# Moving one batch's attention two steps within another batch's feed-forward steps

## The chip, the core and the metric

The kernel runs on one core of a Trainium2 chip. The metric is the device time of one execution in microseconds, given as the median of several runs. The core has five engines that run side by side and wait for each other through semaphores: TensorE (PE in the profile, with its weight loads as PEld), VectorE (DVE), ScalarE (ACT), GpSimd (POOL) and SyncE (SP), which issues most transfers. Each engine works through its own instructions strictly in the order in which the kernel issues them. PSUM is the memory that TensorE writes its results to; SBUF is the large on-chip memory.

## The reference

Two parts follow each other: a cross attention between tokens and a small state, and a feed-forward block with `h * cos(h)` between its two matrices.

```python
# x: (8, 8, 512, 64)  state: (8, 8, 32, 64)
scores = scale * np.matmul(x, state.transpose(0, 1, 3, 2))
a = softmax(scores)                       # over the 32 states
xread = np.matmul(a, state)
scores2 = scale * np.matmul(state, x.transpose(0, 1, 3, 2))
a2 = softmax(scores2)                     # over the 512 tokens
sread = np.matmul(a2, x)
x2 = concatenate([xread, sread], axis=2)  # then (B, H, S, D) -> (B*S, H*D) = (4352, 512)

h = x2 @ w_in                             # (512, 2048)
g = h * np.cos(h)
return g @ w_out                          # (2048, 512)
```

(The softmax is written out in the reference, with the maximum subtracted and 1e-9 added to the sum.)

## The kernel before

The kernel goes through the 8 batches. A batch has 16 steps, one for each *tile* of 128 of the 2048 hidden features (by 512 tokens). In the steps of batch `b` it also does, piece by piece, the attention of batch `b + 1`. A plan says which piece falls into which step. This plan is what the change edits:

```python
        def early(b, s):
            if b == 1:
                ...
            else:
                for k in range(NK):                 # 32x32 transposes of the loaded tokens
                    to = (x_dve, y_dve)[k % 2]
                    to[s[k // 2]].append((b, "tokens_turned", k))
            pe[s[2]].append((b, "scores"))
            x_dve[s[2]].append((b, "max1"))
            x_dve[s[3]].append((b, "spread1"))
            y_dve[s[3]].append((b, "shift"))
            x_dve[s[4]].append((b, "max2"))
            y_act[s[4]].append((b, "exps"))
            x_dve[s[5]].append((b, "sums"))
            y_dve[s[5]].append((b, "spread1"))
            x_dve[s[6]].append((b, "norm1"))

        def late(b, s):
            pairs(s[0], b, "turn", "turn_kept", 0)  # turn a2 on TensorE, copy on ScalarE
            pe[s[1]].append((b, "reads", 0))        # sread
            pe[s[2]].append((b, "reads", 1))
            x_dve[s[2]].append((b, "keep"))
            if len(s) > 3:
                turned(b, s[3])                     # keep2 on TensorE, keep3 on ScalarE
        ... # cut: batch 0
            prod(0, b, 1, *[MAIN for _ in bank])
            prod(4, b, 2, *bank)
            prod(9, b, 3, *bank)
            if b + 1 < B:
                prod(13, b + 1, 0)
                early(b + 1, (1 + (b == 1), 2 + (b == 1), 5, 6, 7, 8, 9))
                late(b + 1, (10, 11, 12, 15))
```

`prod(s, b, nt)` is a *state product*: in step `s`, state times a quarter of `w_in` for batch `b`, 16 passes on TensorE into the two PSUM buffers `at`, copied by ScalarE into the buffer `sw` (two of them in turn). Scores, the turned a2 and the reads use the same two buffers `at`; the scores stay there until `exp2` has read them.

The steps of a batch come in two kinds. From batch 2 on, the hidden products of most tiles are done for two tiles at once with seven products in place of eight (Strassen's scheme; in the trace L514), with sums on VectorE; their result is put together in SBUF. The last 8 steps of an odd batch do one plain product (L471) per tile, which stays in PSUM:

```python
    hps = ctx.enter_context(tc.tile_pool(name="hps", bufs=2, space=PSUM))

    def hidden(t):                                   # L471, plain tile
        t.hp = hps.tile([P, S], F32, name="h")[:, 0:t.n]
        ...
    def gate(t):     # L567, ScalarE: q = int(h + 0.25)
    def gate2(t):    # L570, VectorE: q = q - h
    def gate3(t):    # L573, ScalarE: q = sin(pi/2 - 2 pi q)
    def gate4(t):    # L580, VectorE: g = h * q   (the last reader of h)
```

The feed-forward output is a Strassen scheme too, over pairs of batches. Its sums are the subtractions of L586, some on VectorE and some on GpSimd (all on GpSimd in the first pair, batches 0 and 1). The output products are L624; a step has 4 or 8 passes of them (128x128 by 512), three steps behind the tile. Results leave through 32x32 transposes on VectorE (L651) and transfers.

For a pair's first batch the differences of the attention matrix that the seven products need are made ahead by `halves`:

```python
    def halves(b):                                   # L493
        aT = aT_of[b]
        ...
        for i, x1, x2 in ((0, b12, b11), (1, b22, aS[:, 0]), (2, b22, b12),
                          (3, b21, aS[:, 1])):
            nc.vector.tensor_tensor(aS[:, i], x1, x2, op=ALU.subtract)
```

One step of the loop, cut to its order:

```python
    for step, t in enumerate(all_tiles):
        s = step % NF
        ...
        ahead = all_tiles[step + 1:step + 3]
        if seven(t):
            if t.f % 2 == 0:
                hidden_b(t); sums_b(t)               # second half of a pair
        elif step != 1:
            hidden(t)
        first = len(ahead) > 1 and seven(ahead[0]) and ahead[0].f % 2 == 0
        if first:
            if not seven(t):
                h = t.hp
                take_slot(t)
                nc.scalar.copy(t.g, h)               # L957: frees the PSUM buffer early
            hidden_a(*ahead)                         # first half of the next pair
        ...
            go(0)                                    # pe pieces of the plan
            gate(t); gate2(t)
            if first:
                sums_a(ahead[0])
            go(1); go(3)                             # x_act and x_dve pieces
        gate3(t)
        if later:
            later.pop(0)()                           # a piece of a store
        for u, new in zip(all_tiles[step + 2:step + 4], (False, True)):
            if seven(u) and u.f % 2 == 0 and new_pair(u) == new:
                sw_sums(u)
        gate4(t)
        sums(t)                                      # L586
        go(2); go(4)                                 # y_act and y_dve pieces
        for u in all_tiles[step + 5:step + 6]:
            if seven(u) and new_pair(u):
                halves(u.b)
        sums2(t)                                     # L586 on GpSimd
        while len(line) >= (LAG if step >= 2 * NH else LAG + 1):
            output(line.pop(0))                      # L624
        line.append(t)
```

When `reads(1)` of a batch is issued, the loads of the following batch's tokens are issued too, into the buffer that the reads have just used (`xT`) and into `x_b`.

Of the kernel before, what the change touches and what calls it, by code (L numbers as in the profile page):

```python
# [21 lines left out]
def kernel(  # L22
# [10 lines left out]
    B, H, S, D = x.shape  # L33
# [419 lines left out]
    def part(b, name, *args):  # L453

        if b not in attn:
            attn[b] = Attention(b)
        getattr(attn[b], name)(*args)
        if (name, args) == ("reads", (1,)) and b + 1 < B:
            if b > 0:
                attn[b + 1] = Attention(b + 1)  # L460
                attn[b + 1].load_tokens()
            load_x(b + 1)
# [16 lines left out]
    def seven(t):  # L479
        return t.pair is not None and t.b > 1 and t.phase < 3  # L480
# [35 lines left out]
    def take_slot(t):  # L516
        t.slot = g_free.pop(0)
        t.hp = t.g = g_all[:, t.slot, 0:t.n]
# [253 lines left out]
    def tiles():  # L772
        pr = None
        for b in range(B):
            if b % 2 == 0:
                pr = Pair(b // 2, pr)
            for f in range(NF):
                t = Tile()
                t.b, t.f, t.pair = b, f, pr
                t.phase, t.i = b % 2 * 2 + f // NH, f % NH  # L780
                t.n, t.kn = S, 2
                c = slice(P * f % WC, P * f % WC + P)
                t.lhs = lambda i, b=b, nt=P * f // WC, c=c: (
                    sw_of[b, nt][:, i, c])
                t.rhs = lambda i, b=b: aT_of[b][:, i]
                yield t
        for n in range(NF):
            t = Tile()
            t.b, t.n_th, t.f = B, n, (n + NH) % NF
            t.pair, t.last_pair, t.phase = None, pr, None  # L790
            t.n, t.kn = B * Ns, NK
            cols = slice(P * t.f, P * t.f + P)
            t.lhs = lambda i, cols=cols: w_in[:, i, cols]
            t.rhs = lambda i: sT[:, :, Ns * i:Ns * i + Ns]
            yield t


    def warm(n, to):

        for _ in range(n):  # L800
            nc.tensor.matmul(out=to, lhsT=zeros[:, 0:P], rhs=zeros, start=True,
                             stop=True)
# [33 lines left out]
    def plan(b):  # L836
        pe, x_act, y_act, x_dve, y_dve = [
            {s: [] for s in range(NF)} for _ in range(5)]

        def prod(s, b, nt, *bank):  # L840
            pe[s].append((b, "products", nt) + bank)
            if b == 1 and 0 < nt < 3:
                x_dve[s].append((b, "products_taken", nt) + bank)
            else:
                x_act[s].append((b, "products_kept", nt) + bank)

        def pairs(s, b, name, kept, i):
            pe[s] += [(b, name, i), (b, name, i + 1)]
            x_act[s].append((b, kept, i))
            y_act[s].append((b, kept, i + 1))  # L850

        def early(b, s):
            if b == 1:
                pairs(s[0], b, "tokens", "tokens_kept", 0)
                pairs(s[1], b, "tokens", "tokens_kept", 2)
            else:
                for k in range(NK):
# [13 lines that stand above are left out]
            pairs(s[0], b, "turn", "turn_kept", 0)  # L871
            pe[s[1]].append((b, "reads", 0))
# [3 lines that stand above are left out]
                turned(b, s[3])  # L876

        def turned(b, s):
            pe[s].append((b, "keep2"))
            x_act[s].append((b, "keep3"))  # L880


        if b == 0:
            pe[0].append((0, "products", 0, SIDE, HC, WC))
            y_dve[0] += [(0, "products_taken", 0, SIDE, HC, WC),
                         (0, "inverse2")]
            prod(7, 0, 2, SIDE)
            prod(11, 0, 3)
            prod(13, 1, 0, MAIN)
            late(0, (1, 2, 3, 4))  # L890
            early(1, (5, 6, 7, 8, 9, 10, 11))
            late(1, (12, 13, 14))
        else:
            bank = (SIDE,) if b == 1 else ()
            if b == 1:
                turned(1, 0)
            prod(0, b, 1, *[MAIN for _ in bank])
            prod(4, b, 2, *bank)
            prod(9, b, 3, *bank)
            if b + 1 < B:  # L900
                prod(13, b + 1, 0)
                early(b + 1, (1 + (b == 1), 2 + (b == 1), 5, 6, 7, 8, 9))
                late(b + 1, (10, 11, 12, 15))
        return pe, x_act, y_act, x_dve, y_dve

# [20 lines left out]
    all_tiles = list(tiles())  # L926
    for step, t in enumerate(all_tiles):
        s = step % NF
        if s == 0 and t.b < B:
            steps = plan(t.b)  # L930
        todo = [p[s] if t.b < B else [] for p in steps]

        def go(n):
            for p in todo[n]:
                part(*p)

        last, conv = conv_at.get(step - 1, -1), conv_at.get(step, -1)
        if step == B * NF + (0 if f64 else 8):
            fetch(N_LOADS + 2)
        if step == 4:  # L940
            warm(1, acc[MAIN][0])
# [3 lines that stand above are left out]
                hidden_b(t)  # L945
                sums_b(t)
                if s == NF - 2 and seven(all_tiles[step + 2]):
                    halves(t.b + 1)
# [8 lines that stand above are left out]
                nc.scalar.copy(t.g, h)  # L957
            hidden_a(*ahead)
        if step == 0:
            hidden(all_tiles[1])  # L960
            warm(3, acc[MAIN][0])
            gate(t)
            gate2(t)
            convert(3, "bcdf")
            convert(4, "1")
            go(0)
        else:
            go(0)
            if step == 5:
                states(1, acc[SIDE][1])  # L970
            if not (seven(t) and t.f % 2):
                gate(t)
            gate2(t)
            if step == 3:
                warm(4, acc[MAIN][0])
                part(0, "products", 1, SIDE)
            if first:
                sums_a(ahead[0])
            go(1)
            go(3)  # L980
            if step == 1:
                convert(4, "bcdf")
            elif last >= 0:
                convert(last, "bcdf")
            if conv >= 0 and not todo[1]:
                convert(conv, "1")
        gate3(t)
        if seven(t) and t.f % 2 == 0:
            gate(t.second)
        if step == 3:  # L990
            part(0, "products_kept", 1, SIDE)
        if later:
            later.pop(0)()
# [4 lines that stand above are left out]
        if conv >= 0 and todo[1] and step > 0:  # L998
            convert(conv, "1")
        if t.pair is not None:  # L1000
            sums(t)
        if step == 6:
            states_kept(1, acc[SIDE][1])
        go(2)
        if conv >= 0:
            convert(conv, "2")
        go(4)
        for u in all_tiles[step + 5:step + 6]:
            if seven(u) and new_pair(u):
                halves(u.b)  # L1010
        if step in block_at:
            blocks(*block_at[step])
        if t.pair is not None:
            sums2(t)
# [3 lines that stand above are left out]
# [32 lines left out]
```

## Time and profile before

| | before |
|---|---|
| median of 3 runs | 766.38 us |
| lowest and highest run | 765.16 and 791.84 us |
| profiled run (span of its trace) | 765.96 us (764.2 us) |
| TensorE's clock in the trace | 1.00 of full speed (mean 0.997) |
| busy: TensorE, VectorE, ScalarE, GpSimd | 751.7, 520.3, 316.3, 249.3 us |

[...]

How to read the rows: a row of the view in order of time begins with the start in us from the beginning of the execution and the duration of the row in us; `x4` are four instructions or passes merged into one row; in square brackets stands the idle time of the engine before the row, and the instruction that ended it. L numbers are lines of the kernel. The end of a matrix product is modelled: TensorE takes the next product before it, so a row's duration is a little longer than the distance to the next row.

The steps of batch 3 in this profile: the pair of steps 6 and 7 starts on TensorE at 283.70, the plain tiles of steps 8, 9, 10 and 11 at 296.52, 299.95, 304.95 and 310.32. Batch 5 is the same 167.3 us later. Batch 1 ends, and batch 2's first pair begins, at 168.89.

### The profile page before, as it was taken

The numbers are of one execution on the slowest core, as the hardware profiler recorded it, in microseconds if no ns is written. First come the engines' busy times: TensorE is split into PE (matmuls) and PEld (weight loads), VectorE is DVE, ScalarE is ACT, GpSimd is POOL, SyncE is SP. The second block draws the span as 40 slices with busy tenths as digits, with TensorE's granted clock in tenths as the row PEclk, the third lists the DMA queues.
The fourth block names the chain that finished last, engine by engine and source line by source line (L and its number), as shares of the span: only waits on it lengthen the run. The fifth ranks groups of instructions, "written<-read, shape, count | busy, mean of one in ns | idle before, by whom it ended". The sixth has DMA issues, their size and how long they took to land.

```text
span 764.2 us, 8416 instructions
## 1 busy us (share of the span) xinstructions
PE 751.7 (98%) x2880; PEld 380.4 (50%) x2880; DVE 520.3 (68%) x862; ACT 316.3 (41%) x523; POOL 249.3 (33%) x258
## 2 busy tenths in 40 slices
PE   8998999999999999999999999999999999999997
PEld 3443443445555554445555553445555554455554
DVE  5778777836896788847886789747878676432431
ACT  3887844533254335333362335333443333212212
POOL 2354278777121210662221111751211206500200
PEclk9999999999999999999999999999999999999999
DMA  8595461050002510340105210420100115000021
GB/s 247 170 274 209 131 98 29 4 107 1 14 15 49 90 28 4 54 82 0 29 1 97 41 28 15 70 54 1 27 1 1 28 28 138 0 0 15 14 42 41
DMA packets 161962, 43.54 MB, mean 57 GB/s; under 512 B 153920, under 2 KB 153920, under 8 KB 161920
## 3 DMA queue, kind: packets, MB, share of 16 engines
q1 hardware_dynamic: 161024, 42.49, 25.7%
q10 hardware_dynamic: 768, 0.39, 0.2%
q8 instruction: 23, 0.38, 0.2%
q14 instruction: 19, 0.16, 0.1%
q0 software_dynamic: 128, 0.13, 0.1%
HBM read 34.08 MB, written 8.91 MB: 56 GB/s over the span
## 4 chain that ended last, share of the span: by engine, by line
PE 87%; DVE 7%; ACT 2%; issue 1%; DMA 1%; POOL 1%; SPq 0%; DVEq 0%; ACTq 0%; POOLq 0%
PE o L624 47%; PE h L514 14%; PE h L471 14%; PE at L319 4%; PE o L744 4%; PE at L409 2%; DVE xT L339 1%; PE o L319 1%; DVE q L570 1%; DVE g_all L580 1%; DVE i L333 1%; DMA g_all<-in_moe_w_in_dram 1%; ACT q L567 1%; PE at L392 1%; DVE aT L356 1%
## 5 line engine op out<-in xcount | busy, mean ns | idle before, releaser
L624 PE MATMUL o<-g_all,w_out 128*128 128x512 f32 x512 | 236.4, 598 | 0.4 <-POOL w_out L242 0.4
L624 PE MATMUL o<-g_all,s 128*128 128x512 f32 x384 | 177.3, 598 | 0.0
L586 POOL TENSOR_TENSOR g_all<-g_all 128x512 f32<-128x512 f32 x80 | 112.8, 1433 | 121.2 <-DVE g_all L580 121.2
L624 PEld LDWEIGHTS o<-g_all,w_out 128*128 128x128 f32 x512 | 93.8, 190 | 113.1 <-issue 108.4
L573 ACT ACTIVATE q<-q,halfpi 128x512 f32<-128x512 f32 (+1 forms) x144 | 100.8, 700 | 95.8 <-DVE q L570 95.6
L624 PEld LDWEIGHTS o<-g_all,s 128*128 128x128 f32 x384 | 70.8, 190 | 88.1 <-issue 82.1
L570 DVE TENSOR_TENSOR q<-q,h 128x512 f32<-128x512 int32 (+1 forms) x69 | 42.9, 621 | 103.6 <-ACT q L567 103.6
L471 PE MATMUL h<-aT,sw 128*128 128x512 f32 x224 | 107.2, 602 | 4.8 <-DVE g_all L580 4.3
L567 ACT ACTIVATE q<-g_all 128x512 int32<-128x512 f32 x75 | 46.8, 624 | 141.8 <-DVE g_all L560 141.4
L567 ACT ACTIVATE q<-h 128x512 int32<-128x512 f32 (+1 forms) x69 | 37.6, 545 | 131.0 <-PE h L471 131.0
L570 DVE TENSOR_TENSOR q<-q,g_all 128x512 f32<-128x512 int32 x75 | 52.7, 703 | 35.5 <-ACT q L567 35.5
L471 PEld LDWEIGHTS h<-aT,sw 128*128 128x128 f32 x224 | 41.8, 190 | 60.2 <-issue 45.0
L509 POOL TENSOR_TENSOR swS<-sw 128x128 f32<-128x128 f32 x35 | 17.4, 496 | 148.6 <-PE h L514 107.3
L580 DVE TENSOR_TENSOR g_all<-g_all,q 128x512 f32<-128x512 f32 x75 | 54.0, 720 | 14.5 <-ACT q L573 14.4
L580 DVE TENSOR_TENSOR g_all<-h,q 128x512 f32<-128x512 f32 (+1 forms) x69 | 42.8, 621 | 23.5 <-ACT q L573 23.1
L242 POOL TENSOR_TENSOR w_out<-w_out,s 128x1024 int32<-128x1024 int32 x10 | 23.9, 2390 | 77.6 <-DVE w_out L237 73.4
L509 POOL TENSOR_TENSOR swS<-sw,swS 128x128 f32<-128x128 f32 x35 | 18.3, 522 | 87.4 <-PE h L514 86.9
L514 PEld LDWEIGHTS h<-aT,sw 128*128 128x128 f32 x144 | 27.4, 190 | 34.4 <-issue 28.0
L514 PE MATMUL h<-aS,sw 128*128 128x256 f32 x144 | 43.1, 381 | 0.1
L514 PE MATMUL h<-aS,swS 128*128 128x256 f32 x144 | 42.8, 379 | 0.0
L514 PE MATMUL h<-aT,sw 128*128 128x256 f32 x144 | 42.8, 379 | 0.0
L586 DVE TENSOR_TENSOR g_all<-g_all 128x512 f32<-128x512 f32 x48 | 33.5, 697 | 1.6
(107 smaller groups left out, 886.3 us busy)
## 6 DMA issues: line engine op xcount, KB each, us to landing
out_dram<-ot SPq DMA_DIRECT2D x132, 64.0 KB, 2.0
g_all<-in_moe_w_out_dram SPq DMA_DIRECT2D x8, 1024.0 KB, 5.0
g_all<-in_moe_w_in_dram SPq DMA_DIRECT2D x6, 1024.0 KB, 5.3
xT<-in_x_dram SPq DMA_DIRECT2D x96, 64.0 KB, 2.3
x_b<-in_x_dram SPq DMA_DIRECT2D x24, 256.0 KB, 4.5
x_b<-in_x_dram SPq DMA_DIRECT2D x16, 128.0 KB, 3.8
g_all<-in_moe_w_in_dram SPq DMA_DIRECT2D x4, 512.0 KB, 5.9
x_b<-in_moe_w_out_dram SPq DMA_DIRECT2D x1, 1024.0 KB, 6.1
```

What stands on the lines that cost most here:

```text
L242: nc.gpsimd.tensor_tensor(bits, bits, e, op=ALU.add)
L319: nc.tensor.matmul(out=(to or at)[j][Ns * k:Ns * k + Ns, 0:n], lhsT=w[D * j:D * j + D, self.b, Ns * k:Ns * k + Ns], rhs=r(slice(D * j, D * ...
L471: nc.tensor.matmul(out=t.hp, lhsT=t.lhs(i), rhs=t.rhs(i), start=(i == 0), stop=(i == t.kn - 1))
L509: engine.tensor_tensor(o, x1, x2, op=op)
L514: nc.tensor.matmul(out=out, lhsT=w, rhs=r, start=True, stop=True)
L567: nc.scalar.activation(t.q.bitcast(I32), t.hp, func=ACTF.Copy, bias=0.25)
L570: nc.vector.tensor_tensor(t.q, t.q.bitcast(I32), t.hp, op=ALU.subtract)
L573: nc.scalar.activation(t.q, t.q, func=ACTF.Sin, bias=halfpi, scale=-TWO_PI)
L580: nc.vector.tensor_tensor(t.g, t.hp, t.q, op=ALU.mult)
L586: engine.tensor_tensor(out, a, b, op=ALU.subtract)
L624: nc.tensor.matmul(out=acc[bank][ch], lhsT=w[:, i, P * ch:P * ch + P], rhs=g.g, start=(i == 0), stop=(i == NH - 1))
L744: nc.tensor.matmul(out=acc[MAIN][i], lhsT=t.g[:, P * i:P * i + P], rhs=w_out[:, :, t.f, :], start=(t.n_th == 0), stop=(t.n_th == NF - 1))
```

## The change

In batches 3 and 5 the attention of the next batch runs two steps later from its scores on, which moves its work on VectorE and ScalarE toward the later steps. The buffers `at` hold the scores until the exponentials, so the third state product of the batch moves from step 9 to step 6 and the next batch's first from 13 to 11, ahead of and behind that time. In batch 7, which has no next batch, the third product moves along. In batches 4 and 6 the transposes of the loaded tokens come one step later, because those loads are now issued later. Since the attention matrix is ready two steps later, `halves` is issued two steps later too; this line holds for the first batch of every pair, so also for batch 2, whose attention stays where it was in batch 1.

```diff
@@ -896,10 +896,18 @@
                 turned(1, 0)
             prod(0, b, 1, *[MAIN for _ in bank])
             prod(4, b, 2, *bank)
-            prod(9, b, 3, *bank)
-            if b + 1 < B:
+
+
+            fourth = b % 2 == 1 and b > 1
+            prod(6 if fourth else 9, b, 3, *bank)
+            if fourth and b + 1 < B:
+                prod(11, b + 1, 0)
+                early(b + 1, (1, 2, 7, 8, 9, 10, 11))
+                late(b + 1, (12, 13, 14, 15))
+            elif b + 1 < B:
                 prod(13, b + 1, 0)
-                early(b + 1, (1 + (b == 1), 2 + (b == 1), 5, 6, 7, 8, 9))
+                first = 1 + (b % 2 == 1 or b > 2)
+                early(b + 1, (first, first + 1, 5, 6, 7, 8, 9))
                 late(b + 1, (10, 11, 12, 15))
         return pe, x_act, y_act, x_dve, y_dve
 
@@ -1005,7 +1013,7 @@
         if conv >= 0:
             convert(conv, "2")
         go(4)
-        for u in all_tiles[step + 5:step + 6]:
+        for u in all_tiles[step + 3:step + 4]:
             if seven(u) and new_pair(u):
                 halves(u.b)
         if step in block_at:
```

Nothing is added or taken away; the instructions of the changed kernel are those of the kernel before in another order.

## The prediction

> **What bounds the kernel now.** I read the page's busy table first, then the waits of TensorE, then TensorE's, VectorE's and ScalarE's instructions in order of time around each wait, and last the chain of waits at the border of batches 1 and 2.
>
> ```profile
> PE 751.7 (98%) x2880; PEld 380.4 (50%) x2880; DVE 520.3 (68%) x862; ACT 316.3 (41%) x523; POOL 249.3 (33%) x258
> ```
>
> TensorE (PE) is busy for all but 764.2 - 751.7 = 12.5 us. The change keeps every matrix product, so only idle time of TensorE is to be won. Its waits:
>
> ```profile
> PE h L471 <- DVE g_all L580: 4.3, 6, 1.9
> PE at L801 <- DVE g_all L119: 1.5, 1, 1.5
> ```
>
> Of the 4.3 us on VectorE's line 580, two waits lie in batch 0, outside the change. The other four are two pairs, one in batch 3 and one in batch 5, alike to 0.01 us:
>
> ```profile
> 304.95 1.98 PE L471 MATMUL h<-aT,sw 128*128 128x512 f32 x4 [0.18 <-DVE g_all L580]
> 306.77 1.04 PE L392 MATMUL at<-ident,xT 128*128 128x128 f32 x8
> 307.65 1.88 PE L624 MATMUL o<-g_all,s 128*128 128x512 f32 x4
> 310.32 1.98 PE L471 MATMUL h<-aT,sw 128*128 128x512 f32 x4 [0.79 <-DVE g_all L580]
> ...
> 472.24 1.98 PE L471 MATMUL h<-aT,sw 128*128 128x512 f32 x4 [0.18 <-DVE g_all L580]
> ...
> 477.61 1.98 PE L471 MATMUL h<-aT,sw 128*128 128x512 f32 x4 [0.79 <-DVE g_all L580]
> ```
>
> These are steps 10 and 11. The hidden product needs one of the two PSUM buffers of the pool `hps`, and the buffer of the tile two steps earlier is free only when `gate4` (L580) has read it. A resumed product also runs 0.1 us longer (1.98 against 1.88), so a batch loses 0.97 us of wait and 0.2 of restarts. VectorE is late there because of the attention:
>
> ```profile
> 301.23 0.69 DVE L570 TENSOR_TENSOR q<-q,h 128x512 f32<-128x512 int32 x1 [1.06 <-ACT q L567]
> 301.83 1.30 DVE L333 TRANSPOSE_TENSOR_REDUCE i<-aT 128x16 f32<-128x512 f32 x2
> 303.17 0.18 DVE L375 TENSOR_SCALAR i<-i 128x34 f32<-128x34 f32 x1
> 303.38 0.37 DVE L376 RECIPROCAL i<-i 128x34 f32<-128x34 f32 x1
> 303.67 0.65 DVE L651 STREAM_TRANSPOSE ot<-held 128x512 f32<-128x512 f32 x1
> 304.25 0.65 DVE L580 TENSOR_TENSOR g_all<-h,q 128x512 f32<-128x512 f32 x1
> ```
>
> The second place that matters has no wait worth a row; I found it in the chain at the end of batch 1:
>
> ```profile
> 164.63 0.70 DVE q L570
> 165.32 0.02 issue
> 165.35 0.73 ACT q L573
> 166.08 0.04 DVEq L580
> 166.12 0.04 issue
> 166.16 0.70 DVE g_all L580
> 166.86 0.07 issue
> 166.93 2.50 POOL g_all L586 x2
> 169.43 0.59 ACT g_all L957
> 170.02 0.04 issue
> 170.06 1.13 PE h L514 x4
> ```
>
> Read it backwards: TensorE's third product of batch 2's first pair starts when ScalarE has emptied an `hps` bank (L957), which starts when GpSimd has done two subtractions of tile 14, which start when VectorE's `gate4` of tile 14 ends. TensorE already loses some 0.3 us here. VectorE has no slack before that `gate4`: whatever delays L570 at 164.63 delays TensorE.
>
> [...] The four subtractions of `halves` (L493, two SBUF inputs) take 0.42 us each with GpSimd quiet, but 0.81, 1.37, 1.49 and 1.49 at 147.68 in batch 1, where GpSimd subtracts without a break; L580, with one input in PSUM, keeps its 0.7. [...] The trace has 1.28 us at 297.02 (to Exp) and 1.28 at 301.21 (back to Sin), so the exponentials block ScalarE for 3.58 us from the start of the first load to the next `gate`.
>
> **The change part by part.** No instruction is added or removed. Four moves:
>
> 1. *Batches 3 and 5, the attention of batch b+1.* Scores go from step 5 to 7, the exponentials from 7 to 9, norm1 from 9 to 11, and the third and first state products from 9 and 13 to 6 and 11. I rebuild batch 3 by the instruction order of the changed kernel with durations of the trace. TensorE: without the scores of step 5 the pair of step 5, at 283.70, and four output passes take 1.72 each, so the pair of step 6 starts at 287.14. Then 1.30 (pair) + 1.11 (state product with its switch) + 3.54 (8 passes after it) + 1.11 (scores) + 3.54 gives 297.74 for hidden(8). From there hidden and one output product alternate, 1.72 each: hidden(9) at 301.18, hidden(10) at 304.62, hidden(11) would be at 308.06. VectorE: hidden(8) can be read at 297.74 + 1.88 = 299.62, gate 0.1 later takes 0.63, so L570 of tile 8 starts at 300.35. By start-to-start times follow 0.60 (L570), 1.16 (spread, L339), 0.63 (store transpose), 0.69 (L580), 0.61 (L586), 1.20 (shift), 0.60 (L570 of tile 9), 1.33 + 0.08 (max2), 0.63 (store transpose), 0.65 (L580): 8.18 us, so `gate4` of tile 9 ends near 308.5. hidden(10) needs `gate4` of tile 8, done at 303.4: no wait. hidden(11) waits 308.5 - 308.06, about 0.5 us. One step on: ScalarE's Exp section starts near 306.7, so the gate of tile 10 is at 306.7 + 3.58 = 310.3, VectorE then needs 0.63 + 0.60 + 1.34 + 0.50 + 0.65 and is done at 314.0; hidden(12) comes at about 308.55 + 1.82 + 1.11 + 3.54 = 315.0. No wait, because from step 11 a step has 8 output passes in place of 4. The state product of step 11 writes the buffers that exp2 reads until 310.3, and comes at 310.5: just free. So 0.97 + 0.2 become 0.5 + 0.1: a gain of 0.57 us a batch, 1.1 us in both.
>
> 2. *Batches 4 and 6: token transposes one step later* (four of 0.7 us, from steps 1 and 2 to 2 and 3). Two of them now delay VectorE by 1.25 us in step 3, behind the sums that TensorE needs next. After it VectorE idles 0.76 + 0.29 + 1.44 us until 370.48 waiting for others. Absorbed: 0.
>
> 3. *Loads of the next tokens later*, with reads(1), from step 12 to 14. In the kernel before, 16 issues ran from 313.40 to 327.57 and then four of x. Shifted by some 10.5 us they end near 338, and landing takes 2.3 us; the transposes come at about 356. Absorbed: 0.
>
> 4. *`halves` two steps later for every pair, also in batch 1*, where the attention does not move. There the four subtractions leave step 11, where nobody waited for them, and come right behind `gate4` of tile 13, which ends at 161.49. GpSimd starts its three subtractions of tile 13 at 161.64. By issue order the first of the four runs free (0.42) [...]: 1.3 + 1.4 + 1.4 from the row at 147.68. They end near 161.42 + 4.5 = 165.9. L570 of tile 14, which ran at 164.63, is then 1.3 us late, and so through the chain shown above are L580, GpSimd, L957 and TensorE: a loss of 1.3 us. In batches 3 and 5 the same move is harmless: GpSimd has two subtractions a step, the reads lie in steps 13 and 14, and by the same count `halves` ends near 330.0, just when the gate of tile 14 (ready near 329.8) is needed.
>
> Sum: -1.1 + 0 + 0 + 1.3 = +0.2 us, 0.03% of the span. Batch 7 only has its third state product at step 6; no wait is near.
>
> **The rivals.** (a) *The stalls of batches 3 and 5 vanish and batch 1 keeps its slack*: -2 x 1.17 = -2.3 us, some 764. For it: from step 11 on TensorE's steps are longer. Against it: my count puts hidden(11) still in a step of 4 output passes, and the order of the instructions does put `halves` before L570 of tile 14. (b) *The stall is only moved*: exponentials, store transposes and both reductions meet steps 9 and 10, and 0.97 us comes back whole, while batch 1 loses 1.3: some 767.5. My margins of 0.2 us at the state product and 1.0 at hidden(12) are thin enough for it. (c) *The contention in batch 1 costs little*: [...] `halves` ends before 164.6 and nothing is lost: -1.1 us, 765. The block of four at 147.68 speaks against it. (d) *A late transfer*: late tokens would hold VectorE in order, several us. Some 15 us of slack speak against it.
>
> **Range and chances.** The three timed runs before have the median 766.38 and the lowest 765.16; the profiled run took 765.96. I predict the middle of these plus 0.2, 766.0 us. Rivals (a) and (b) span 764 to 767.5, and the runs themselves scatter by about 1 us, so 764.3 to 767.7 should hold 8 times in 10. A gain of 2% is 15 us, more than all idle time of TensorE: 0.5%. A loss of 2% would need a stall of 15 us, which only rival (d) or a disturbed measurement could give: 1.5%.
>
> **What would show it.** Right: the list of TensorE's waits has one wait of about 0.5 us on `gate4` in each of batches 3 and 5, at step 11, and none at step 10; L493 near 161.4 reads about 0.4, 1.3, 1.4, 1.4; L570 of tile 14 starts near 166; the product of `sw` and `aS` that started at 170.06 starts near 171.4. Wrong: no waits in batches 3 and 5, or two; L493 at 0.42 in batch 1; a wait of VectorE on a transfer at L301; a TensorE wait on ScalarE at the state product of step 11.

## The result, and the profile after

| | before | after |
|---|---|---|
| median | 765.86 us (4 runs) | 770.23 us (4 runs) |
| span of the profiled execution | 764.2 us | 768.2 us |
| ratio of the runs, 95% interval | | 1.0064 [1.0044, 1.0084] |

The changed kernel is slower by 0.4 to 0.8%, and lies outside the predicted range. One of the four runs before, of 791.84 us, lies 3.5% above the fastest, counts as slow, and is left out of the ratio (770.23 / 765.33). (Over 42 later runs the kernel before has a median of 765.90.)

The page's busy table and TensorE's waits of the changed kernel (waiter, what released it, us in total, times, the longest):

```profile
PE 752.2 (98%) x2880; PEld 380.4 (50%) x2880; DVE 521.4 (68%) x862; ACT 316.2 (41%) x523; POOL 250.2 (33%) x258
```

```profile
PE o L624 <- DVE held L637: 3.8, 2, 1.9
PE h L471 <- DVE g_all L580: 3.2, 4, 1.9
...
PE at L801 <- DVE g_all L119: 1.5, 1, 1.5
...
PE o L624 <- POOL w_out L242: 0.4, 1, 0.4
PE h L514 <- POOL sw L509: 0.3, 1, 0.3
...
```

Every engine is as busy as before, to about 1 us. The waits on L580 are down by 1.1 us, as the change intended. Two lie in the steps that the change touches and are new: 3.8 us on L637, a line that no wait had named, and 0.3 us on GpSimd's L509.

TensorE in batch 3, in order of time (batch 5 has the same two waits):

```profile
307.95 1.98 PE L471 MATMUL h<-aT,sw 128*128 128x512 f32 x4 [0.43 <-DVE g_all L580]
309.87 1.09 PE L319 MATMUL at<-w_in,st_all 64*32 64x512 f32 x16
310.88 2.96 PE L624 MATMUL o<-g_all,s 128*128 128x512 f32 x6
315.75 1.12 PE L624 MATMUL o<-g_all,s 128*128 128x512 f32 x2 [1.91 <-DVE held L637]
```

and VectorE at the same time:

```profile
310.18 0.69 DVE L570 TENSOR_TENSOR q<-q,h 128x512 f32<-128x512 int32 x1 [1.55 <-ACT q L567]
310.78 1.30 DVE L333 TRANSPOSE_TENSOR_REDUCE i<-aT 128x16 f32<-128x512 f32 x2
312.11 0.18 DVE L375 TENSOR_SCALAR i<-i 128x34 f32<-128x34 f32 x1
312.33 0.37 DVE L376 RECIPROCAL i<-i 128x34 f32<-128x34 f32 x1
312.61 0.63 DVE L580 TENSOR_TENSOR g_all<-h,q 128x512 f32<-128x512 f32 x1
313.28 0.69 DVE L586 TENSOR_TENSOR g_all<-g_all 128x512 f32<-128x512 f32 x1
313.89 1.24 DVE L339 STREAM_TRANSPOSE xT<-i 128x1024 f32<-128x1024 f32 x1
315.05 0.65 DVE L637 TENSOR_SCALAR held<-o 128x512 f32<-128x512 f32 x1
```

L637 is half of `keep_product`: when the third output product of a pair of batches is complete, in step 10, ScalarE and VectorE each copy one of its two PSUM banks away (`MAIN`). In step 11 the output products of the first plain tile start a new sum in the same banks, and with the seventh of the eight passes they meet the bank that VectorE has not yet read. VectorE has the copy at the end of a queue: `gate2` (L570), the sums of the moved attention (L333, L375, L376), `gate4`, a subtraction, the spread of the sums (L339), and only then L637, done at 315.70. TensorE had been ready at 313.84.

Where the time went shows best in how much later TensorE stands at the same product. The rows are those of L514 on `swS` and `aS` (rounded, so that a difference can be off by 0.01):

| product | before | after | later by | so this stretch adds |
|---|---|---|---|---|
| first pair of batch 2 | 169.32 | 167.98 | -1.34 | |
| second pair of batch 2 | 181.81 | 181.07 | -0.74 | +0.60 |
| fourth pair of batch 2 | 202.15 | 201.47 | -0.68 | +0.06 |
| first pair of batch 4 | 336.83 | 337.63 | +0.80 | +1.49 |
| first pair of batch 6 | 504.12 | 508.10 | +3.98 | +3.18 |
| end of the span | 764.2 | 768.2 | +4.0 | 0 |

The -1.34 at the start is no gain of the change: TensorE's clock was at 0.50 from 73.68 to 77.10 in the profile of before and not in this one. Batch 5 is batch 3 over again (+1.49) and then 1.7 us more, with a lowered clock (last section). So the change itself costs 0.66 + 2 x 1.49 = 3.6 us, and its long waits bring lowered clocks on top.

### The profile page after: what moved, and what is told of

The parts are those of the page before. It is cut to its first block, busy times and chain, and to the rows that moved or that the text cites. A ratio compares the mean times of both kernels' runs of the same rounds, so it can differ in the third digit from the quotient of the medians.

```text
span 768.2 us, 8413 instructions
## 1 busy us (share of the span) xinstructions
PE 752.2 (98%) x2880; PEld 380.4 (50%) x2880; DVE 521.4 (68%) x862; ACT 316.2 (41%) x523; POOL 250.2 (33%) x258
## 4 chain that ended last, share of the span: by engine, by line
PE 87%; DVE 6%; ACT 2%; issue 2%; POOL 1%; DMA 1%; SPq 0%; ACTq 0%; DVEq 0%; POOLq 0%
PE o L624 48%; PE h L471 14%; PE h L514 14%; PE at L319 4%; PE o L744 4%; PE at L409 2%; DVE xT L339 1%; PE o L319 1%; PE at L392 1%; DMA g_all<-in_moe_w_in_dram 1%; DVE i L333 1%; ACT q L567 1%; DVE aT L356 1%; DVE q L570 1%; DVE g_all L580 1%
## 5 line engine op out<-in xcount | busy, mean ns | idle before, releaser
L624 PE MATMUL o<-g_all,w_out 128*128 128x512 f32 x512 | 237.0, 600 | 0.4 <-POOL w_out L242 0.4
L624 PE MATMUL o<-g_all,s 128*128 128x512 f32 x384 | 177.6, 597 | 3.8 <-DVE held L637 3.8
L586 POOL TENSOR_TENSOR g_all<-g_all 128x512 f32<-128x512 f32 x80 | 113.7, 1445 | 127.9 <-DVE g_all L580 125.0
L624 PEld LDWEIGHTS o<-g_all,w_out 128*128 128x128 f32 x512 | 93.4, 190 | 115.8 <-issue 111.2
L570 DVE TENSOR_TENSOR q<-q,h 128x512 f32<-128x512 int32 (+1 forms) x69 | 43.0, 623 | 109.2 <-ACT q L567 109.2
L624 PEld LDWEIGHTS o<-g_all,s 128*128 128x128 f32 x384 | 70.9, 190 | 90.4 <-issue 79.5
L570 DVE TENSOR_TENSOR q<-q,g_all 128x512 f32<-128x512 int32 x75 | 54.5, 726 | 36.0 <-ACT q L567 36.0
L580 DVE TENSOR_TENSOR g_all<-g_all,q 128x512 f32<-128x512 f32 x75 | 55.0, 733 | 16.2 <-ACT q L573 16.1
L509 POOL TENSOR_TENSOR swS<-sw 128x128 f32<-128x128 f32 x35 | 17.3, 495 | 145.4 <-PE h L514 106.1
L580 DVE TENSOR_TENSOR g_all<-h,q 128x512 f32<-128x512 f32 (+1 forms) x69 | 42.7, 619 | 18.4 <-ACT q L573 17.1
L509 POOL TENSOR_TENSOR swS<-sw,swS 128x128 f32<-128x128 f32 x35 | 18.3, 523 | 87.5 <-PE h L514 87.0
L514 PEld LDWEIGHTS h<-aT,sw 128*128 128x128 f32 x144 | 27.4, 190 | 34.4 <-issue 28.0
L514 PE MATMUL h<-aS,sw 128*128 128x256 f32 x144 | 43.2, 381 | 0.5 <-POOL sw L509 0.3
L514 PE MATMUL h<-aS,swS 128*128 128x256 f32 x144 | 42.8, 379 | 0.0
L514 PE MATMUL h<-aT,sw 128*128 128x256 f32 x144 | 42.8, 379 | 0.0
L586 DVE TENSOR_TENSOR g_all<-g_all 128x512 f32<-128x512 f32 x48 | 33.2, 692 | 1.6
```

What stands on the lines that cost most here:

```text
L509: engine.tensor_tensor(o, x1, x2, op=op)
L514: nc.tensor.matmul(out=out, lhsT=w, rhs=r, start=True, stop=True)
L570: nc.vector.tensor_tensor(t.q, t.q.bitcast(I32), t.hp, op=ALU.subtract)
L580: nc.vector.tensor_tensor(t.g, t.hp, t.q, op=ALU.mult)
L586: engine.tensor_tensor(out, a, b, op=ALU.subtract)
L624: nc.tensor.matmul(out=acc[bank][ch], lhsT=w[:, i, P * ch:P * ch + P], rhs=g.g, start=(i == 0), stop=(i == NH - 1))
```

## The experiments

Each kernel ran 5 to 22 times, beside the kernel before. "Steps" are the stretches of the table above: border of batches 1 and 2, batch 3, batch 5. A step of +3.18 holds a lowered clock of TensorE.

| run | median, us | ratio to before, 95% interval | steps, us |
|---|---|---|---|
| after | 770.23 | 1.0064 [1.0044, 1.0084] | +0.66, +1.49, +3.18 |
| e1: copy on ScalarE | 765.58 | 0.9994 [0.9986, 1.0002] | +0.66, -0.69, -0.69 |
| e2: `halves` of batch 2 back | 769.69 | 1.0057 [1.0040, 1.0073] | 0, +3.18, +3.18 |
| e3: both | 765.04 | 0.9986 [0.9979, 0.9993] | 0, -0.70, -0.69 |
| e4: spread behind the copy | 766.94 | 1.0016 [1.0008, 1.0025] | +0.67, +0.36, +0.36 |
| e5: before, copy on ScalarE | 766.49 | 1.0004 [0.9996, 1.0012] | 0, 0, +0.29 |
| e6: before, `halves` of batch 2 late | 766.07 | 1.0008 [1.0000, 1.0016] | +0.66, 0, 0 |
| e7: before, stores behind `gate4` | 766.15 | 0.9998 [0.9990, 1.0007] | 0, 0, 0 |
| e8: both, stores behind `gate4` | 767.26 | 1.0019 [1.0013, 1.0026] | 0, +0.31, +0.33 |
| e9: both, two stores put off | 762.91 | 0.9967 [0.9955, 0.9979] | 0, -1.28, -1.29 |
| e10: before, two stores put off | 762.97 | 0.9969 [0.9957, 0.9980] | 0, -1.20, -1.20 |
| e11: after, wait filled | 769.51 | 1.0059 [1.0046, 1.0072] | +0.67, +1.99, +1.98 |

**e1, the copy taken from VectorE.** (The diffs of this part are shortened; the `#` comments in them are not in the kernels.)

```diff
+        if act:                    # pairs 1 and 2, third output product
+            nc.scalar.activation(out.t[:, 1], acc[bank][1], func=ACTF.Copy,
+                                 scale=TWO_PI)
+            return
         nc.vector.tensor_scalar(out.t[:, 1], acc[bank][1], TWO_PI, None,
```

> The changed kernel, with the second half of the copy out of the MAIN accumulator (L637, VectorE) moved to ScalarE in pairs 1 and 2. Theory (TensorE waits 1.91 us in step 11 of batches 3 and 5 because that copy stands behind the attention's reduction and spread on VectorE): both waits go, 2 x (1.91 + 0.1) = 4.0 us less than the changed kernel, some 766.2 us against 770.2. Rival (VectorE as a whole is the bound of steps 9 to 12): only the 0.6 us of work that leaves VectorE is won, 1.2 us in both, and the rest comes back as a wait on L580 in step 12: some 769. Second rival (the loss is ScalarE's, the exponentials being late): more work on ScalarE makes it worse, over 770.5.

The wait on L637 is gone, and nothing took its place. TensorE's longest waits of e1:

```profile
PE h L471 <- DVE g_all L580: 3.2, 4, 1.9
PE at L805 <- DVE g_all L119: 1.5, 1, 1.5
...
PE h L471 <- ACT sw L445: 0.5, 1, 0.5
PE h L514 <- POOL sw L509: 0.3, 1, 0.3
```

A batch gains 1.49 + 0.69 = 2.2 us, over three times the 0.6 us of work that left VectorE. Neither VectorE's amount of work nor ScalarE's lateness was the cause; ScalarE even took work on.

**e4, the copy left on VectorE, one place earlier.** This is the sharper test, for no engine has less to do:

```diff
-            y_dve[s[5]].append((b, "spread1"))
+            (x_dve[s[6]] if b in (4, 6) else y_dve[s[5]]).append(
+                (b, "spread1"))
             x_dve[s[6]].append((b, "norm1"))
```

> The changed kernel, with the second spread (L339, 1.16 us on VectorE) issued behind the copy L637 in place of ahead of it in batches 3 and 5; no work is taken from any engine. Theory (the place in VectorE's order is the cause): L637 ends 1.16 us earlier, the wait shrinks from 1.91 to about 0.75 us, 2 x 1.16 = 2.3 us less, some 767.9. Rival (VectorE's amount of work is the bound): nothing changes, 770.2, the wait of 1.9 us turning into waits on L580 in steps 12 and 13.

TensorE's row of e4 that answers to 315.75 of after:

```profile
315.96 1.13 PE L624 MATMUL o<-g_all,s 128*128 128x512 f32 x2 [0.78 <-DVE held L637]
```

1.91 became 0.78: the difference of 1.13 us is the spread's place in the queue (1.16 from start to start). Batch 3's stretch fell from 1.49 to 0.36, by the same 1.13. The time is 1.0 us better than expected; in this profile, with waits of 0.78 us, the clock stayed at 1.00 in batches 3 and 5, which fits (last section).

**e5, the control.** The edit of e1 on the kernel before.

> The kernel before the change, with the same copy L637 moved to ScalarE in pairs 1 and 2: the control of the first repair. Theory (in the kernel before this copy comes when nobody waits for it, only the moved attention put it on the path): no change, 765.9 us, the two waits per batch on L580 stay at 0.18 and 0.79. Rival (the copy is better on ScalarE in any order): 764.5 or less.

Nothing gained (interval up to 0.04% faster, 0.12% slower); in batch 5 one wait on L580 even grew from 0.18 to 0.46 (why is not shown). The rows of the kernel before at that place:

```profile
313.25 3.70 PE L624 MATMUL o<-g_all,s 128*128 128x512 f32 x8
```

```profile
313.83 0.68 DVE L637 TENSOR_SCALAR held<-o 128x512 f32<-128x512 f32 x1
```

There L637 is done at 313.83 + 0.68 = 314.5, and TensorE's eight passes of that step begin at 313.25, so that the last two, at 0.43 us a pass, need the bank near 315.8. Only the moved attention put the copy on the path.

**e2 and e6, `halves` of batch 2.** e2 takes that part of the change back, e6 does that part alone.

```diff
-        for u in all_tiles[step + 3:step + 4]:      # e6: step + 5:step + 6
-            if seven(u) and new_pair(u):
+        for u, b2 in zip(all_tiles[step + 3:step + 6:2], (False, True)):   # e6: (True, False)
+            if seven(u) and new_pair(u) and (u.b == 2) == b2:
                 halves(u.b)
```

> The changed kernel, with the differences for batch 2 (halves, L493) back in step 11 of batch 1, and only those. Theory (in step 13 they [...] delay gate4 of tiles 14 and 15 and GpSimd's subtractions, and so the sums of sw that TensorE waits for at 180.5): the wait of 0.33 us on GpSimd's L509 goes, 0.6 us less, some 769.6. Rival (that wait is chance, the 0.6 us come from elsewhere): the wait stays and the time is 770.2.

> The kernel before the change, with nothing but the differences for batch 2 (halves, L493) moved from step 11 to step 13 of batch 1: that part of the change alone. Theory: a wait of 0.33 us on GpSimd's L509 appears near 182, and 0.66 us are lost, some 766.6. My prediction's step (TensorE waits for ScalarE's copy of tile 15, 1.3 us lost at 170): 767.2, with the product of sw and aS at 171.4. Rival (no cost by itself): 765.9.

Both say the same: 0 with `halves` in step 11, +0.66 with it in step 13, in every kernel that has it there. The run times alone could not settle 0.66 us (e6's interval touches 1); the traces do. VectorE, GpSimd and ScalarE of the changed kernel at that place:

```profile
159.47 0.68 DVE L580 TENSOR_TENSOR g_all<-h,q 128x512 f32<-128x512 f32 x1
160.07 0.42 DVE L493 TENSOR_TENSOR aS<-aT 128x256 f32<-128x256 f32 x1
160.53 1.37 DVE L493 TENSOR_TENSOR aS<-aT,aS 128x256 f32<-128x256 f32 x1
161.82 1.48 DVE L493 TENSOR_TENSOR aS<-aT 128x256 f32<-128x256 f32 x1
163.22 1.48 DVE L493 TENSOR_TENSOR aS<-aT,aS 128x256 f32<-128x256 f32 x1
164.63 0.68 DVE L570 TENSOR_TENSOR q<-q,h 128x512 f32<-128x512 int32 x1
166.15 0.69 DVE L580 TENSOR_TENSOR g_all<-h,q 128x512 f32<-128x512 f32 x1 [0.84 <-issue]
169.60 1.58 DVE L570 TENSOR_TENSOR q<-q,g_all 128x512 f32<-128x512 int32 x1 [2.76 <-ACT q L567]
...
172.71 0.68 DVE L580 TENSOR_TENSOR g_all<-g_all,q 128x512 f32<-128x512 f32 x1
```

```profile
166.92 3.72 POOL L586 TENSOR_TENSOR g_all<-g_all 128x512 f32<-128x512 f32 x3 [2.49 <-DVE g_all L580]
173.54 3.74 POOL L586 TENSOR_TENSOR g_all<-g_all 128x512 f32<-128x512 f32 x3 [2.90 <-PE o L624]
177.22 0.91 POOL L509 TENSOR_TENSOR swS<-sw 128x128 f32<-128x128 f32 x1
```

```profile
168.08 0.59 ACT L965 COPY g_all<-h 128x512 f32<-128x512 f32 x1 [2.02 <-PE h L471]
```

and the rows of the kernel before that answer to the last ones:

```profile
169.42 0.59 ACT L957 COPY g_all<-h 128x512 f32<-128x512 f32 x1 [3.35 <-POOL g_all L586]
```

```profile
170.94 0.69 DVE L570 TENSOR_TENSOR q<-q,g_all 128x512 f32<-128x512 int32 x1 [4.09 <-ACT q L567]
...
173.16 0.68 DVE L580 TENSOR_TENSOR g_all<-g_all,q 128x512 f32<-128x512 f32 x1
```

```profile
173.99 3.74 POOL L586 TENSOR_TENSOR g_all<-g_all 128x512 f32<-128x512 f32 x3 [3.34 <-DVE g_all L580]
```

The four L493 take 0.42, 1.37, 1.48 and 1.48 us, as predicted, and hold L570 of tile 14 until 164.63. It stood there in the kernel before too, but here TensorE is 1.34 us earlier, so L570 is some 1.3 us late. The copy L965 (L957 before), however, starts at 168.08, while GpSimd's second subtraction, begun at 166.92 and two times 1.24 long, ends at 169.4. The copy does not wait for that subtraction. The delay takes another road: L570 of the next tile, at 169.60, now begins before GpSimd is done with its three subtractions (166.92 + 3.72 = 170.64) and takes 1.58 us; in the kernel before it begins at 170.94, behind them (166.93 + 3.72 = 170.65), and takes 0.69. That delays `gate4` (L580) and with it GpSimd's next three subtractions, which start 5.99 us after the pair's first product in place of 5.10. (GpSimd's row at 173.54 names L624 as what released it. That product ended within 0.02 us of `gate4`; but in the kernel before GpSimd starts at the same 0.15 us behind `gate4`, and well before that row of L624 ends.) Behind the three stand the sums of `sw` that the second pair of batch 2 needs. There TensorE waits 0.33 us for L509. The last row of this road in e6 (the row in the changed kernel is at 180.53):

```profile
183.64 0.70 PE L514 MATMUL h<-aS,sw 128*128 128x256 f32 x2 [0.33 <-POOL sw L509]
```

**e3, both repairs.**

> The changed kernel with both repairs. If the two losses are separate and add: 770.2 - 4.0 - 0.6 = 765.6 us, about 0.3 to 1 us below the kernel before, with one wait of 0.43 us on L580 left in each of batches 3 and 5. Rival (VectorE bound): some 768.5.

The steps add exactly (0, -0.70, -0.69), and the time is below that of the kernel before: 0.9986 [0.9979, 0.9993]. So the idea of the change is worth some 1.4 us by the trace and 1.1 by the runs; two side effects hid it. The wait of 0.43 us on `gate4` of tile 9 is left.

**e7 and e8, a store piece behind `gate4` in every step.** A failed attempt on the waits that are left.

```diff
-        if later:
-            later.pop(0)()
         for u, new in zip(all_tiles[step + 2:step + 4], (False, True)):
             ...
         gate4(t)
+        if later:
+            later.pop(0)()
```

> The kernel before the change, with a piece of a store (L651, 0.6 us on VectorE) issued behind gate4 of its step in place of ahead of it, in all steps. Theory (TensorE waits in steps 10 and 11 for gate4, and the store transpose stands in front of it): of 0.97 us of wait and 0.2 of restarts per batch some 0.55 and 0.1 remain, 1.0 us less, some 764.9. Rival (the store only changes place with the subtraction behind it, and the later gate4 is as late as before): 765.9.

> The changed kernel with both repairs and the store pieces behind gate4. Theory: the one wait left in batches 3 and 5 (0.43 us on gate4 of tile 9) goes, and a short one on the exponentials (at, about 0.2 us) may take its place: 0.6 us less than with both repairs, some 764.4, the fastest of all. Rival: other steps lose by the later stores what these win, 765.0 or more.

e7 gains nothing: the waits of batch 3 shrink to one of 0.78, but in step 4 TensorE now waits 0.20 us for L546, at a cost of 0.43. e8 is 1.0 us a batch worse than e3 (+0.31 against -0.70). It pays the same 0.43 in step 4, a wait of 0.30 is left in step 11, and there the state product takes 1.56 us from its start to the next product in place of 1.01: it waits for the exponentials (L365) to have read `at`, and these begin at 308.19 in place of 307.29 in e3. VectorE and GpSimd of e8 show where the order broke:

```profile
303.07 0.65 DVE L580 TENSOR_TENSOR g_all<-h,q 128x512 f32<-128x512 f32 x1
303.65 0.69 DVE L655 STREAM_TRANSPOSE ot<-held 128x512 f32<-128x512 f32 x1
304.26 1.35 DVE L586 TENSOR_TENSOR g_all<-g_all 128x512 f32<-128x512 f32 x1
```

```profile
303.81 1.26 POOL L586 TENSOR_TENSOR g_all<-g_all 128x512 f32<-128x512 f32 x1 [22.60 <-DVE g_all L580]
```

With the transpose (L655 here) between them, L586 comes when GpSimd has already begun on the same tile, and takes 1.35 us in place of 0.69. Directly behind `gate4` it had come first, as in e3:

```profile
304.03 0.69 DVE L586 TENSOR_TENSOR g_all<-g_all 128x512 f32<-128x512 f32 x1
```

```profile
304.08 3.01 POOL L586 TENSOR_TENSOR g_all<-g_all 128x512 f32<-128x512 f32 x2 [23.10 <-DVE g_all L580]
```

**e9 and e10, only the two store pieces that are in the way**, put off from steps 8 and 9 to 11 and 12 of batches 3 and 5.

```diff
-        if later:
+        if later and not (t.b in (3, 5) and s in (8, 9, 10)):
             later.pop(0)()
```

> The changed kernel with both repairs, and the two store pieces (L651) that stand ahead of gate4 in steps 8 and 9 of batches 3 and 5 put off to steps 11 and 12. Theory (the last wait, 0.43 us on gate4 of tile 9, is VectorE's order again; 1.2 us of transposes leave the front of it): the wait and its restart go, 0.53 us a batch, and 1.4 + 1.06 = 2.4 us below the kernel before, some 763.5. Rival (the exponentials, which the next state product waits for, set the same time): the wait moves to the state product of step 11, no gain over both repairs, 765.0.

> The kernel before the change with the same two store pieces put off from steps 8 and 9 of batches 3 and 5, the attention unmoved. Theory (the waits of 0.18 and 0.79 us are a matter of VectorE's order, and 0.6 and 1.2 us leave the front of the two gate4): both waits and restarts go, 2 x 1.17 = 2.3 us, some 763.6: the aim of the change without moving the attention. Rival (gate4 of tile 9 is late for ScalarE's sake): the first wait goes, the second stays, 765.3.

In both, no row of TensorE's in batches 1 to 7 shows a wait any more; of its waits on L580 only the two of batch 0 are left. So the rival of e9, that the wait would move to the state product of step 11, did not come. The row of e10:

```profile
PE h L471 <- DVE g_all L580: 2.4, 2, 1.9
```

Both beat the kernel before by 0.3%, and they can't be told apart (0.9967 [0.9955, 0.9979] and 0.9969 [0.9957, 0.9980]). e10 does it with the attention unmoved: one condition on a queue reaches what the change was made for.

**e11, the long wait filled.** Two products whose result is not used stand in front of the waiting one.

```diff
+            if pr.n in (1, 2) and i == 0:
+                for _ in range(2):
+                    nc.tensor.matmul(out=at[0], lhsT=ident, rhs=w_in[:, 0, 0:WC],
+                                     start=True, stop=True)
             product(MAIN, s2, pr.b[0, i], i)
```

> The changed kernel with two idle products of 128x512 (identity by weights, into a buffer that is overwritten next, 1.7 us) in the place where TensorE waits 1.9 us for L637 in batches 3 and 5. No other work changes. Theory (a wait of 1.9 us lowers TensorE's granted clock to 0.50 for some 3.4 us in most executions, 1.7 us more): the clock stays 1.00 in batches 3 and 5, the position of TensorE behind the wait is the same as with a full clock, and the time is 770.2 less one to two times 1.7, some 767.5. Rival (the lowered clock is unrelated to the wait): clock drops go on, 770.2.

TensorE of e11 at that place:

```profile
313.94 1.98 PE L731 MATMUL at<-w_in,ident 128*128 128x512 f32 x4 [0.81 <-ACT sw L445]
315.76 1.88 PE L624 MATMUL o<-g_all,s 128*128 128x512 f32 x4
```

The filling itself waited 0.81 us and made each stretch 0.5 us longer (1.99 against 1.49). The clock stayed at 1.00 in both batches, and the time is not above that of the changed kernel, though TensorE had 1.0 us more to do. That fits the theory and falls short of its number (767.5 expected, 769.51 measured; the longer stretches are 1.0 us of the difference). Three of e11's five runs have a mean clock of 1.000, while none of the changed kernel's four is above 0.998. This supports the theory and does not prove it; the last section goes on from here.

## Why the prediction was wrong, step by step

- *Part 1, batches 3 and 5, VectorE's `gate4` in steps 10 and 11*: right. Predicted no wait at step 10 and about 0.5 us at step 11; measured none and 0.43. With that alone a batch gains 0.69 (e1, e3), where I had 0.57.
- *Part 1, "hidden(12) comes at about 308.55 + 1.82 + 1.11 + 3.54 = 315.0. No wait, because from step 11 a step has 8 output passes in place of 4"*: this step failed. Those 8 passes were counted as free to run, but the last two need a PSUM bank that L637 empties, and L637 stands behind the second spread on VectorE. In the trace the term of 3.54 us is 5.84 (310.88 to 316.72). e1 and e4 show that it is this copy's place in the order. So each of batches 3 and 5 has two waits, as the prediction named for a sign of being wrong. I had followed `hps` and `at` from writer to last reader, and not the output banks: the profile of before names no wait on them, since there the copy came early enough. The 2.2 us between -0.69, the stretch without this wait, and +1.49, twice, are most of the miss.
- *Parts 2 and 3, token transposes and loads later: absorbed, 0*: right. From batch 4's first pair to the end of batch 5's seven-product steps TensorE's position changes by 0.02 us, and no wait of TensorE or VectorE on these loads appears.
- *Part 4, `halves` in batch 1, 1.3 us lost through L957*: the times of L493 came as counted (0.42, 1.37, 1.48, 1.48 against 0.4, 1.3, 1.4, 1.4), but the link to TensorE was wrong. I took "ScalarE's copy starts when GpSimd has done two subtractions" from a coincidence of 0.01 us in one trace. In both kernels the copy at this place starts 0.37 us after the end of its own product (169.05 to 169.42 before, 167.71 to 168.08 after), wherever GpSimd stands, and in batches 3 and 5 it starts 0.09 us after it (336.56 to 336.65, 337.37 to 337.46). (Why it takes 0.28 us longer at the end of batch 1 is open.) The delay came out 10 us later, through the sums of `sw`, and cost 0.66.
- *Rivals*: (b), the stall is only moved, was nearest, but for a reason I had not given: not `gate4`, an accumulator. (a) is what e9 reached by other means. (c) was half right, by luck: L493 was not faster than counted, but it cost 0.66 in place of 1.3. (d) did not occur.
- *Range*: it held only stalls that I had found. A reordering also moves what stands behind the moved pieces (one spread put behind the copy, in e4, shortened the wait on it by 1.13 us), so the range should have kept room for a reader I had not followed.

The sum of the prediction was -1.1 + 1.3 = +0.2. With what the runs showed it is -2 x 0.69 + 2 x 2.18 + 0.66 = +3.6 us, before lowered clocks.

## What to carry to other kernels

When work moves within the order of one engine, list every buffer whose last reader stands behind the moved pieces in the new order, accumulator banks included, and check each against the time at which it is written next; a wait that the profile does not name today is the likeliest one tomorrow. Where an end and a start agree to 0.01 us in one place, look at a second instance of the same instruction before building on it as a cause. And before moving a large piece to make room, try to move the small ones that stand in front of the critical instruction: two transposes put off three steps gave all that two steps of attention were meant to give.

## What the runs showed of the hardware that was not expected

**A lowered clock of TensorE followed 11 of 17 waits of 1.9 us.** Windows of 3 us of the changed kernel around the wait in batch 5 (busy time and count of each engine, then the granted clock, the share of DMA and GB/s):

```profile
482.00:485.00 3.00, 1.09 (x3) 0.30 (x2) 2.96 (x6) 0.89 (x2) 2.90 (x2) 1.00 0.00 0
485.00:488.00 3.00, 3.00 (x6) 1.28 (x5) 2.50 (x4) 0.72 (x1) 1.22 (x2) 0.64 0.00 0
488.00:491.00 3.00, 3.00 (x12) 1.79 (x11) 0.69 (x1) 1.97 (x4) 1.88 (x2) 0.79 0.00 0
491.00:494.00 3.00, 3.00 (x8) 1.33 (x7) 1.39 (x2) 0.41 (x1) 2.21 (x2) 1.00 0.02 5
```

Soon after the wait, from 485.84 to 489.25, the clock is at 0.50, which costs 1.7 us here and about 1.35 behind the wait in batch 0 of the kernel before. In the thirteen traces a wait of 1.9 us occurs 17 times: one in batch 0 of each, and four on L637. A lowered clock followed 11 of them, 3 of the 4 on L637. It followed none of the waits of 0.9 us or less, and occurred nowhere else but in the last 2 us of an execution. (The record of the clock begins 5.4 us into the trace of before and 4.6 us into that of the changed kernel.)

In the traces of both kernels the changes of the clock lie whole multiples of 3.413 us apart: in the changed kernel 141 of them from the beginning of the record to the fall, 1 to the rise, 82 to the next fall; in the kernel before 20, 1 and 201. The four waits of 1.9 us of these two traces lie differently against these multiples, counted from the falls at 485.84 and 73.68:

| wait | from, to | stretch of 3.41 us | TensorE idle in it | clock behind it |
|---|---|---|---|---|
| after, batch 5 | 482.62, 484.53 | 482.43 to 485.84, holds the whole wait | 56% | 0.50 |
| before, batch 0 | 71.08, 73.03 | 70.27 to 73.68, holds the whole wait | 57% | 0.50 |
| after, batch 0 | 71.11, 73.06 | 69.41 to 72.83, ends within the wait | 50% | 1.00 |
| after, batch 3 | 313.84, 315.75 | 311.75 to 315.17, ends within the wait | 39% | 1.00 |

What sets the clock, and whether there is a limit between 50 and 56%, these four waits do not show.

So a wait of 1.9 us cost its length and, where a lowered clock followed it, 1.35 to 1.7 us more. The same shows in the run times: those of e1, which has one such wait, fall into two groups (six up to 764.9, seven from 765.6), and the mean clock recorded with each run is 0.999 or 1.000 in the first and 0.997 or 0.998 in the second.

**Two subtractions at the same time: L586 on VectorE took 0.69 us or 1.35.** It takes 0.69 in e3, where it starts 0.05 us ahead of GpSimd's subtraction, and 1.35 in e8, where one transpose in between lets GpSimd start 0.45 us ahead of it (rows under e8).
